# Low halves of the expert weights: summed by TensorE through identity matrices instead of subtracted by GpSimd, with eighteen places for raw slices

## The chip, the core and the metric

The kernel runs on one core of a Trainium2 chip. The metric is the device time of one execution in microseconds (us); smaller is better. Engines are named as in the profile: PE is TensorE (PEld its weight loads), DVE is VectorE, ACT is ScalarE, POOL is GpSimd, and SP is the engine whose queue issues most of the transfers.

## What is computed

There are two parts, one behind the other. The first is a linear recurrence with a complex decay for 4 batches, 8 heads, 768 steps and a head width of 48. The second is a two-layer network on the 3072 tokens that come out of it.

```python
mag = np.sqrt(a_re * a_re + a_im * a_im)
scale = np.minimum(mag, 0.999) / (mag + 1e-06)
...
for t in range(S):
    S_re, S_im = (ar * S_re - ai * S_im) + k_t v_t^T, ar * S_im + ai * S_re
    y[:, :, t] = q_t S_re
...
h = x @ w_in                      # 3072 x 384 by 384 x 2048
g = np.maximum(0.01 * h, h)
return g @ w_out                  # 3072 x 2048 by 2048 x 384
```

The two weight matrices come as 64-bit floats. The kernel converts them on the chip, and it wants about fp32 accuracy from matmuls in the `fp32r` type, which keeps fewer bits of a number. So every operand of the network is split in two, a high part `hi` in `fp32r` and a low part `lo` = value - `hi`, and each product is the sum of three: hi times hi, hi times lo, lo times hi.

## The kernel before

**The two stages.** Time is cut into 6 chunks of 128 steps, and each chunk into 2 pairs of batches: 12 sub-blocks `n`. For each one `prep(n)` builds the decayed queries and keys on DVE and ACT, from the raw tiles `a`, `qk` and `v`: normalising the decay (L468 to L484), products within groups of 8 steps (L489, L492, seven rounds), a scan over groups (L499 to L513), and the multiplication into `qkt` (L533 to L584). Transfers (L600 to L608) then turn `qkt` into the layout `t96` that TensorE needs (rows call it `t`). `attend` has four pieces for each sub-block, two for each batch: scores (`att<-t`, masked by DVE at L670 into `asb`) and the update of the running state, which ends in `xh` (ACT, L698) and `xl` (DVE, L701), the two halves of the network's input.

**The network.** `stream(g)` handles 256 tokens in 8 steps of 256 hidden columns. `first(g, s)` is 18 matmuls into `ph`; ACT (L752) and DVE (L753) make the leaky ReLU `tg`, ACT rounds it to `gh` (L754), DVE makes the remainder `gl` (L755). `second(g, s)` is 18 matmuls into `po`. The network of sub-block n-1 is laid out in one row of 16 or 18 steps, and the four attention pieces of sub-block n stand behind its steps 6, 8, 10 and 12. TensorE works through this row strictly in order, so a piece whose `t` is late stops the network matmuls behind it too.

**The weights.** There are 32 slices of 128 by 384, 16 of `w_in` and 16 of `w_out`, taken in turn. A slice is loaded raw (`stage_...<-in_w_dram`, 64 bits a number) into one of nine places, which are borrowed from tiles that are needed only later (`a`, `kn`, `xh`, `xl`, `stg`); from the ninth slice on the last three places rotate. Then `load_weights` does this with it:

- DVE L424 (`wcv<-stage`) shifts the upper word, DVE L428 puts the sign back: the number as an fp32 bit pattern, without its last 3 bits;
- ACT L431 takes these 3 bits from the lower word, and POOL L432 adds them;
- ACT L433 rounds the result to `fp32r` (`win_hi`, `wout_hi`), and POOL L434 subtracts that from it (`win_lo`, `wout_lo`).

`wcv` has two buffers. In the program's order the slices are spread over the preparation of sub-blocks 0, 1 and 2 on DVE. The order on each engine is set by a scheduler from priorities and a timeline of its own; TensorE's matmuls of the two stages keep the order in which they were written.

Of the kernel before, what the change touches and what calls it, by code (L numbers as in the profile page):

```python
# [9 lines left out]
I32 = mybir.dt.int32  # L10
U32 = mybir.dt.uint32
I64 = mybir.dt.int64
AF = mybir.ActivationFunctionType
# [7 lines left out]
P = 128  # L21
# [22 lines left out]

GAP = 2
TAIL = [1]
STAGES = [
    ("a", 3 * TI * 2 * C, 2), ("kn", H * 2 * D, 1), ("xh", TI * GT, 2), ("xl", TI * GT, 2), ("xh", TI * GT, 2),
    ("xl", TI * GT, 2), ("stg", 2 * DM, 1),
]  # L50
AHEAD = 4
EARLY = 8


def STAGE_OF(i):
    return i if i < 9 else 6 + i % 3

# [223 lines left out]
def body(ctx, tc, keep, a_in, qk_in, v_in, w_in, out):  # L281
# [23 lines left out]
    wacc = keep.tile([P, 2, WCP * -(-NWC // WCK)], F32, tag="wacc", name="wacc")  # L305

    def mm(out, **kw):
        tc.keep_in_program_order(nc.tensor.matmul(out, **kw))  # L308

    prio(PRIO_PREP)  # L310
    nc.scalar.preload_act_table_set("natural_log_exp_and_others")
    make_identity(nc, ident)


# [91 lines left out]
    def load_weights(lo, hi, base):  # L406
        prio(base)
        for f in range(lo, hi):
            for s in (f, NFC + f):
                i = s_next[0]  # L410
                st = weight_dma(i)
                cv = pp.tile([P, DM], I32, tag="cvt", name=f"wcv_{s}", bufs=2)
                s_next[0] += 1
                if s < NFC:
                    dh = win_hi[:, :, f * P : (f + 1) * P]
                    dl = win_lo[:, :, f * P : (f + 1) * P]
                else:
                    dh = wout_hi[:, f].rearrange("p (k x) -> p k x", k=TI)
                    dl = wout_lo[:, f].rearrange("p (k x) -> p k x", k=TI)
                words = st.rearrange("p (x two) -> p x two", two=2)  # L420
                uwords = st.bitcast(U32).rearrange("p (x two) -> p x two", two=2)
                hi_w, lo_w = words[:, :, 1], words[:, :, 0]
                wf = cv.bitcast(F32).rearrange("p (k x) -> p k x", k=TI)
                nc.vector.tensor_scalar(  # L424
                    out=cv.bitcast(U32), in0=uwords[:, :, 1], scalar1=5, scalar2=2,
                    op0=ALU.logical_shift_left, op1=ALU.logical_shift_right,
                )
                nc.vector.scalar_tensor_tensor(  # L428
                    out=hi_w, in0=hi_w, scalar=-(1 << 30), in1=cv, op0=ALU.bitwise_and, op1=ALU.bitwise_or
                )  # L430
                nc.scalar.activation(lo_w, uwords[:, :, 0], AF.Copy, scale=2.0**-29)  # L431
                nc.gpsimd.tensor_tensor(out=cv, in0=hi_w, in1=lo_w, op=ALU.add)  # L432
                nc.scalar.activation(dh, wf, AF.Copy)  # L433
                nc.gpsimd.tensor_tensor(out=dl, in0=wf, in1=dh.bitcast(F32), op=ALU.subtract)  # L434

# [196 lines left out]
    def attend(n, bi):  # L632
# [10 lines left out]
        def turn(hh):  # L643
            pt = att_bank()
            for h4 in range(4):
                tc.keep_in_program_order(
                    nc.tensor.transpose(
# [146 lines left out]
    for n in range(nsub + 1):  # L794
# [10 lines left out]
        if n > 0:  # L805
            order = stream(n - 1)
            for i, (what, g, s) in enumerate(order):
                what(g, s)
                left = len(order) - 1 - i
                while pieces and left <= GAP * len(pieces) + TAIL[min(n, len(TAIL) - 1)]:  # L810
                    pieces.pop(0)()
                    if left > 0:
                        break
                if n == nsub and left == 3:
                    prio(PRIO_FLAG)
                    bad = flag(nc, keep, pp, att_bank(), acc, zfl, wacc, xacc, low)
        for p in pieces:
            p()
    prio.save()
# [78 lines left out]
```

## Time and profile before

| what | value |
|---|---|
| time, median of 3 runs | 679.23 us (675.53 to 681.4) |
| the profiled execution's own time | 679.77 us, span 678.0 us |
| PE busy | 544.5 us, 80% of the span |
| DVE busy | 548.2 us, 81% |
| ACT busy | 368.6 us, 54% |
| POOL busy | 83.3 us, 12% |
| waits of PE for the transfer of `t`, whole span | 85.7 us, the first of them 73.0 us |

A share of the whole span is a mean over stages with different limits: PE has almost nothing to do in the first 79 us, and then works almost without a gap from 182 us on. So the page's row of forty slices, and the busy time by stage, say more than the totals. A duration in the timeline overlaps that of the next instruction on the same engine a little; the distance from start to start is what an instruction costs its engine.

### The profile page before, as it was taken

Reading aid. Unit: us, or ns where it says so; the run is one execution under the profiler, and the core shown is the slowest. Engines: PE = TensorE matmul, PEld = TensorE weight load, DVE = VectorE, ACT = ScalarE, POOL = GpSimd, SP = SyncE. Lnnn points to the kernel's source line nnn. Section 1 sums busy time; section 2 is a strip of 40 time slices with the busy share of each in tenths; the row PEclk is TensorE's granted clock in tenths of the full one; section 3 lists DMA queues with packets and bytes.
Section 4 is the critical chain, followed back from the end, with each engine's and each line's share of the span. In section 5 each row is a group of like instructions: output and inputs, shape, how many; then the busy total and the mean of one; then the engine's idle time right before and its main releaser. Section 6 shows DMA issues by size and latency. Waiting matters only on the chain.

```text
span 678.0 us, 17666 instructions
## 1 busy us (share of the span) xinstructions
PE 544.5 (80%) x7554; PEld 526.7 (78%) x7554; DVE 548.2 (81%) x917; ACT 368.6 (54%) x827; POOL 83.3 (12%) x75
## 2 busy tenths in 40 slices
PE   1000256668899999999999999999969998889996
PEld 0000245558899999999999999998969998889995
DVE  5989899979989999999998989979969876224231
ACT  6335166437557466574755747547446555657221
POOL 5665344541000000000000000000000000000000
PEclk9999977969999999999999999999989999999998
DMA  9223643370541603517045090370640763783000
GB/s 351 72 71 105 185 152 121 102 202 3 125 138 52 192 22 95 169 53 180 34 102 161 3 255 10 114 149 3 176 87 2 220 205 106 214 276 114 24 1 29
DMA packets 26246, 79.22 MB, mean 117 GB/s; under 512 B 3376, under 2 KB 9520, under 8 KB 26160
## 3 DMA queue, kind: packets, MB, share of 16 engines
q1 hardware_dynamic: 25552, 76.43, 38.3%
q10 hardware_dynamic: 608, 1.59, 1.1%
q8 instruction: 61, 1.00, 0.6%
q14 instruction: 25, 0.20, 0.1%
HBM read 54.26 MB, written 4.72 MB: 87 GB/s over the span
## 4 chain that ended last, share of the span: by engine, by line
DVE 38%; PE 26%; DMA 18%; issue 6%; ACT 6%; POOL 2%; SPq 1%; ACTq 0%; DVEq 0%; POOLq 0%
PE ph L308 11%; PE po L308 11%; DMA t<-qkt 10%; DMA wck<-in_w_dram 5%; PE att L308 4%; DVE tg L753 3%; DVE gl L755 3%; DVE tmp L489 3%; DVE asb L670 2%; DVE qkt L584 2%; DVE wcv L424 2%; DVE a L483 2%; DVE a L538 2%; DVE qkt L572 2%; DVE a L492 2%
## 5 line engine op out<-in xcount | busy, mean ns | idle before, releaser
L308 PE MATMUL ph<-xh,win_hi 128*128 128x256 f32 x576 | 165.2, 287 | 13.5 <-DVE tg L753 13.1
L308 PE MATMUL ph<-xl,win_hi 128*128 128x256 f32 x576 | 164.5, 286 | 3.5 <-DVE xl L701 3.5
L308 PE MATMUL ph<-xh,win_lo 128*128 128x256 f32 x576 | 164.0, 285 | 0.0
L308 PE MATMUL po<-gh,wout_hi 128*128 128x256 f32 x576 | 146.2, 290 | 3.4 <-ACT gh L754 3.4
L308 PE MATMUL po<-gh,wout_lo 128*128 128x256 f32 x576 | 141.4, 282 | 0.0
L308 PEld LDWEIGHTS ph<-xh,win_hi 128*128 128x128 f32 x576 | 110.7, 192 | 15.0 <-DVE tg L753 14.1
L308 PEld LDWEIGHTS po<-gh,wout_hi 128*128 128x128 f32 x576 | 109.8, 191 | 6.1 <-ACT gh L754 3.8
L753 DVE TENSOR_TENSOR tg<-ph,tg 128x512 f32<-128x512 f32 x96 | 65.6, 684 | 59.7 <-ACT tg L752 57.4
L308 PEld LDWEIGHTS ph<-xl,win_hi 128*128 128x128 f32 x576 | 110.8, 192 | 4.0 <-DVE xl L701 4.0
L308 PE MATMUL att<-t 96*32 96x64 f32 (+3 forms) x1536 | 41.4, 261 | 89.2 <-DMA t<-qkt 85.7
L308 PEld LDWEIGHTS ph<-xh,win_lo 128*128 128x128 f32 x576 | 110.8, 192 | 0.0
L308 PEld LDWEIGHTS po<-gh,wout_lo 128*128 128x128 f32 x576 | 109.9, 191 | 0.0
L308 PEld LDWEIGHTS att<-t 96*32 96x32 f32 x1536 | 35.5, 146 | 94.6 <-DVE a L492 73.4
L752 ACT ACTIVATE tg<-ph 128x512 f32<-128x512 f32 x96 | 56.8, 592 | 64.3 <-PE ph L308 63.9
L754 ACT CAST gh<-tg 128x512 fp32r<-128x512 f32 x96 | 59.3, 619 | 51.4 <-DVE tg L753 50.4
L308 PE MATMUL po<-gl,wout_hi 128*128 128x256 f32 x576 | 83.9, 281 | 1.3 <-DVE gl L755 1.3
L755 DVE TENSOR_TENSOR gl<-tg,gh 128x512 fp32r<-128x512 f32 x96 | 67.2, 700 | 12.1 <-ACT gh L754 11.9
L308 PEld LDWEIGHTS po<-gl,wout_hi 128*128 128x128 f32 x576 | 75.1, 190 | 1.7 <-DVE gl L755 1.7
L489 DVE TENSOR_TENSOR tmp<-a 128x384 f32<-128x384 f32 x84 | 51.4, 612 | 1.6
L308 PE MATMUL att<-asb,v 128*32 128x128 f32 x768 | 39.4, 287 | 5.7 <-DVE asb L670 5.7
L670 DVE TENSOR_TENSOR asb<-att,mask 128x512 f32<-128x512 f32 x48 | 32.1, 679 | 7.1 <-PE att L308 7.1
L729 ACT ACTIVATE rst<-rst,t 96x48 f32<-96x48 f32 x128 | 30.7, 323 | 13.1 <-DVE rst L722 13.0
(119 smaller groups left out, 884.0 us busy)
## 6 DMA issues: line engine op xcount, KB each, us to landing
t<-qkt SPq DMA_DIRECT2D x44, 290.2 KB, 6.3
wck<-in_w_dram SPq DMA_DIRECT2D x10, 1152.0 KB, 6.3
v<-in_v_dram SPq DMA_DIRECT2D x12, 832.0 KB, 5.3
a<-in_a_dram SPq DMA_DIRECT2D x12, 768.0 KB, 6.6
qk<-in_qk_dram SPq DMA_DIRECT2D x12, 768.0 KB, 4.6
out_dram<-ot SPq DMA_DIRECT2D x12, 384.0 KB, 4.3
stage_xh<-in_w_dram SPq DMA_DIRECT2D x10, 384.0 KB, 3.4
stage_xl<-in_w_dram SPq DMA_DIRECT2D x10, 384.0 KB, 3.1
```

What stands on the lines that cost most here:

```text
L308: tc.keep_in_program_order(nc.tensor.matmul(out, **kw))
L424: nc.vector.tensor_scalar(out=cv.bitcast(U32), in0=uwords[:, :, 1], scalar1=5, scalar2=2, op0=ALU.logical_shift_left, op1=ALU.logical_shif ...
L483: nc.vector.tensor_tensor(out=a[:, 1:3, sl], in0=a[:, 1:3, sl], in1=two(s0), op=ALU.mult)
L489: nc.vector.tensor_tensor(out=pr, in0=src.unsqueeze(2).to_broadcast([P, 2, 2, M]), in1=swap(ar, r), op=ALU.mult)
L492: nc.vector.tensor_tensor(out=zr[:, :, r], in0=pr[:, 0], in1=pr[:, 1], op=ALU.add)
L538: nc.vector.tensor_tensor(out=zk, in0=zk, in1=over_r(0), op=ALU.mult)
L670: nc.vector.tensor_tensor(out=asb, in0=ps, in1=mask, op=ALU.mult)
L729: nc.scalar.activation(r[:, h // 2, h % 2], src[:, h // 2, h % 2], AF.Copy, scale=t96[:, s0 + x, bi, C : C + 1])
L752: nc.scalar.activation(tg, ph, AF.Copy, scale=0.01)
L753: nc.vector.tensor_tensor(out=tg, in0=ph, in1=tg, op=ALU.max)
L754: nc.scalar.copy(gh, tg)
L755: nc.vector.tensor_tensor(out=gl, in0=tg, in1=gh.bitcast(F32), op=ALU.subtract)
```

## The change

All 32 slices are still split in two, but the sums are made elsewhere.

- POOL has no part in it: L432 and L434 are gone.
- DVE gets one instruction more for each slice (L447 in the changed file): it cuts the fp32 pattern down to its upper 20 bits and writes that over the raw upper word.
- ACT L448 writes the 3 bits of the lower word as one byte into the lowest byte of that same word; ACT L449 makes `hi` from it.
- PE makes the low part in PSUM with three matmuls of 384 columns: the identity (fp32) times the pattern, minus two times the identity (`nid`, fp32r) times `hi`, and the identity (fp32) times the cut pattern with its byte. The tile `pd` takes turns in the three banks that the network's `po` uses later.
- ACT copies `pd` to `win_lo` or `wout_lo` (L455).
- There are 18 places for raw slices, in place of 9: the tiles `qkt` and `t96` are borrowed as well, and the last five rotate. `wcv` has four buffers. `EARLY` goes from 8 to 14, which puts the first 14 slices ahead of the preparation in the order of the code.
- TensorE's matmuls of the two stages are kept in order by a chain of dependences; the new ones are not in that chain. The places of the attention pieces are now written as a table, and it names the steps 6, 8, 10, 12 again.

```diff
-GAP = 2
-TAIL = [1]
+PLACE = [(), (6, 8, 10, 12)]
 STAGES = [
-    ("a", 3 * TI * 2 * C, 2), ("kn", H * 2 * D, 1), ("xh", TI * GT, 2), ("xl", TI * GT, 2), ("xh", TI * GT, 2),
-    ("xl", TI * GT, 2), ("stg", 2 * DM, 1),
+    ("a", 3 * TI * 2 * C, 2), ("kn", H * 2 * D, 1), ("qkt", 4 * TI * 2 * (C + 1), 1), ("t96", 2 * H * 2 * (C + 1), 1),
+    ("xh", TI * GT, 2), ("xl", TI * GT, 2), ("xh", TI * GT, 2), ("xl", TI * GT, 2), ("stg", 2 * DM, 1),
 ]
+NST = 18
+NROT = 5
 AHEAD = 4
-EARLY = 8
+EARLY = 14
...
 def STAGE_OF(i):
-    return i if i < 9 else 6 + i % 3
+    return i if i < NST else NST - NROT + (i - NST) % NROT
...
     def mm(out, **kw):
-        tc.keep_in_program_order(nc.tensor.matmul(out, **kw))
+        chained(nc.tensor.matmul(out, **kw))
 
     prio(PRIO_PREP)
+    nid = cp.tile([P, P], F32R, tag="nid", name="nid")
...
+    nc.scalar.activation(nid, ident, AF.Copy, scale=-2.0)
...
-                cv = pp.tile([P, DM], I32, tag="cvt", name=f"wcv_{s}", bufs=2)
+                cv = pp.tile([P, DM], I32, tag="cvt", name=f"wcv_{s}", bufs=4)
...
-                hi_w, lo_w = words[:, :, 1], words[:, :, 0]
+                hi_w = words[:, :, 1]
+                r8 = st.bitcast(U8).rearrange("p (x b) -> p x b", b=8)[:, :, 4]
+                tf = st.bitcast(F32).rearrange("p (k x two) -> p k x two", k=TI, two=2)[:, :, :, 1]
...
                 nc.vector.scalar_tensor_tensor(
-                    out=hi_w, in0=hi_w, scalar=-(1 << 30), in1=cv, op0=ALU.bitwise_and, op1=ALU.bitwise_or
+                    out=cv, in0=hi_w, scalar=-(1 << 30), in1=cv, op0=ALU.bitwise_and, op1=ALU.bitwise_or
                 )
-                nc.scalar.activation(lo_w, uwords[:, :, 0], AF.Copy, scale=2.0**-29)
-                nc.gpsimd.tensor_tensor(out=cv, in0=hi_w, in1=lo_w, op=ALU.add)
-                nc.scalar.activation(dh, wf, AF.Copy)
-                nc.gpsimd.tensor_tensor(out=dl, in0=wf, in1=dh.bitcast(F32), op=ALU.subtract)
+
+                nc.vector.tensor_single_scalar(hi_w, cv, -(1 << 12), op=ALU.bitwise_and)
+                nc.scalar.activation(r8, uwords[:, :, 0], AF.Copy, scale=2.0**-29)
+                nc.scalar.activation(dh, tf, AF.Copy)
+                pd = pso.tile([P, 512], F32, tag=f"o{i % NOC}", name=f"pd_{s}")[:, 0:DM]
+                pd = pd.rearrange("p (k x) -> p k x", k=TI)
+                nc.tensor.matmul(pd, lhsT=ident, rhs=wf, start=True, stop=False)
+                nc.tensor.matmul(pd, lhsT=nid, rhs=dh, start=False, stop=False)
+                nc.tensor.matmul(pd, lhsT=ident, rhs=tf, start=False, stop=True)
+                nc.scalar.copy(dl, pd)
```

Two places show what this does to the order on the engines. The first is DVE around the last two instructions of `prep(0)`, those that finish `qkt` and let the transfers of `t` go (L584, in the changed file L605). Before:

```order
L483 TENSOR_TENSOR a_282<-a_282,tmp_676 128x1536
L579 TENSOR_TENSOR qk_133<-qk_133,a_132 128x768
L424 TENSOR_SCALAR wcv_345<-stage_xh_129 128x384
L424 TENSOR_SCALAR wcv_353<-stage_xl_130 128x384
L584 TENSOR_TENSOR qkt_244<-qk_133,a_132 128x6x128 x2
L489 TENSOR_TENSOR tmp_676<-a_282 128x384
L428 SCALAR_TENSOR_TENSOR stage_xh_129<-stage_xh_129,wcv_345 128x384
```

Now:

```order
L504 TENSOR_TENSOR a_390<-a_390,tmp_808 128x1536
L443 SCALAR_TENSOR_TENSOR wcv_565<-stage_xh_131,wcv_565 128x384
L600 TENSOR_TENSOR qk_137<-qk_137,a_136 128x768
L443 SCALAR_TENSOR_TENSOR wcv_577<-stage_xl_132,wcv_577 128x384
L439 TENSOR_SCALAR wcv_589<-stage_xh_133 128x384
L439 TENSOR_SCALAR wcv_601<-stage_xl_134 128x384
L447 TENSOR_SCALAR stage_xh_131<-wcv_565 128x384
L510 TENSOR_TENSOR tmp_808<-a_390 128x384
L605 TENSOR_TENSOR qkt_352<-qk_137,a_136 128x6x128 x2
L447 TENSOR_SCALAR stage_xl_132<-wcv_577 128x384
L443 SCALAR_TENSOR_TENSOR wcv_589<-stage_xh_133,wcv_589 128x384
```

In the first order 17 of the 32 first steps (L424) and 15 second steps (L428) stand ahead of the end of `qkt`, and the other slices behind it, as far as the middle of `prep(2)`. In the second all 32 first steps (L439), 30 second steps (L443) and 29 of the new third steps (L447) stand ahead of it, and the last five instructions on weights right behind.

The second place is PE between the transposes of the first attention block (`att<-ident,t`) and the products with the masked scores (`att<-asb,v`). Before:

```order
L647 MATMUL att_99<-ident,t_0_271 128x96 x4
L647 MATMUL att_100<-ident,t_0_271 128x96 x4
L308 MATMUL att_101<-asb_0_0_498,v_134 32x128 x6
```

Now:

```order
L668 MATMUL att_101<-ident,t_0_379 128x96 x4
L668 MATMUL att_102<-ident,t_0_379 128x96 x4
L453 MATMUL pd_595<-win_hi,nid 128x384
L454 MATMUL pd_595<-stage_xh_133,ident 128x384
L453 MATMUL pd_607<-wout_hi,nid 128x384
L454 MATMUL pd_607<-stage_xl_134,ident 128x384
L319 MATMUL att_103<-asb_0_0_630,v_138 32x128 x6
```

`pd_607` is the last slice: 29 of the 32 low parts are summed on PE ahead of the first attention matmul, three end among those of the first batch, and none stands in the network's part of the row, whose order is as before.

## Rows read from the trace of the kernel before

**Rows 1.** The page, busy time of each engine, and DVE in 40 slices of the span (tenths busy).

```profile
PE 544.5 (80%) x7554; PEld 526.7 (78%) x7554; DVE 548.2 (81%) x917; ACT 368.6 (54%) x827; POOL 83.3 (12%) x75
...
DVE  5989899979989999999998989979969876224231
```

**Rows 2.** Busy time by stage: the stretch (us from the span's start), its length, busy us of PE, PEld, DVE, ACT and POOL with numbers of instructions, then PE's granted clock (1.00 is 2.4 GHz, 0.50 is 1.2 GHz), the share of the DMA engines and GB/s.

```profile
6.15:73.00 66.85, 0.04 (x4) 0.00 (x0) 60.45 (x84) 30.99 (x62) 40.27 (x30) 1.00 0.37 131
73.00:106.80 33.80, 15.00 (x306) 12.29 (x306) 30.19 (x53) 17.29 (x48) 13.85 (x14) 0.81 0.61 184
106.80:140.80 34.00, 19.53 (x133) 18.49 (x133) 33.23 (x45) 16.34 (x33) 18.70 (x13) 0.80 0.46 122
140.80:182.00 41.20, 35.44 (x494) 33.37 (x494) 38.09 (x61) 23.49 (x61) 6.93 (x7) 0.91 0.29 94
182.00:560.00 378.00, 368.30 (x5400) 360.48 (x5401) 344.46 (x601) 223.21 (x520) 0.00 (x0) 0.99 0.40 111
```

**Rows 3.** What PE waited for from 100 to 200 us: us in total, times, the longest.

```profile
PE att L308 <- DMA t<-qkt: 10.6, 1, 10.6
PE ph L308 <- DVE tg L753: 3.3, 2, 3.2
PE ph L308 <- DVE xl L701: 3.2, 1, 3.2
```

**Rows 4.** The timeline: start, us, engine, line, what was done, and in brackets the idle time before it and what ended it. The last writes to `qkt` of sub-block 0, the first scores, the first full run of network matmuls, the first scores of sub-block 1.

```profile
71.22 1.81 DVE L584 TENSOR_TENSOR qkt<-qk,a 128x768 f32<-128x768 f32 x2
...
79.16 0.61 PE L308 MATMUL att<-t 96*32 96x128 f32 x8 [72.97 <-DMA t<-qkt]
...
106.79 0.58 PE L308 MATMUL ph<-xl,win_hi 128*128 128x256 f32 x1 [3.15 <-DVE xl L701]
...
140.09 0.64 PE L308 MATMUL att<-t 96*32 96x128 f32 x8 [10.55 <-DMA t<-qkt]
```

**Rows 5.** Groups of DVE instructions, busy us in total and mean ns of one. The first two rows are from 6 to 73 us, the others from 182 to 560 us.

```profile
L489 DVE TENSOR_TENSOR tmp<-a 128x384 f32<-128x384 f32 x8 | 7.4, 930 | 0.1
...
L428 DVE SCALAR_TENSOR_TENSOR stage_xl<-stage_xl,wcv 128x384 int32<-128x384 int32 x4 | 2.2, 547 | 0.0
...
L489 DVE TENSOR_TENSOR tmp<-a 128x384 f32<-128x384 f32 x61 | 33.7, 553 | 1.2
...
L506 DVE TENSOR_TENSOR tmp<-xs 128x360 f32<-128x360 f32 (+3 forms) x36 | 16.6, 462 | 2.7 <-ACT xs L498 1.5
...
L538 DVE TENSOR_TENSOR a<-a 128x1536 f32<-128x1536 f32 x9 | 15.8, 1752 | 0.0
...
L512 DVE TENSOR_TENSOR xs<-tmp 128x90 f32<-128x90 f32 (+3 forms) x36 | 8.4, 232 | 0.9
```

**Rows 6.** The timeline of DVE, two neighbours each, at moments when POOL does nothing.

```profile
70.68 0.35 DVE L424 TENSOR_SCALAR wcv<-stage_xh 128x384 uint32<-128x384 uint32 x1
70.95 0.35 DVE L424 TENSOR_SCALAR wcv<-stage_xl 128x384 uint32<-128x384 uint32 x1
...
204.28 0.95 DVE L539 TENSOR_TENSOR a<-a,qkt 128x768 f32<-128x768 f32 x1
205.15 0.95 DVE L540 TENSOR_TENSOR a<-a,qkt 128x768 f32<-128x768 f32 x1
```

**Rows 7.** What DVE waited for up to 110 us (the longest entry), and one POOL instruction of the timeline.

```profile
DVE wcv L424 <- POOL win_lo L434: 5.5, 3, 2.3
...
44.21 5.49 POOL L432 TENSOR_TENSOR wcv<-stage_xl 128x384 int32<-128x384 int32 x1 [2.23 <-issue]
```

**Rows 8.** Records of PE. The first three are fp32 matmuls of 128 columns (ns shortest/median/longest, first and last start in us; each instruction of the program leaves two records). The others are from the timeline (start, us): the network's fp32r matmuls of 256 columns, one record each, and one of their weight loads.

```profile
L341 PE MATMUL att<-perm x32: 420/421/421, 4.3 to 5.8; 128*32 128x128 f32 x32
...
L308 PE MATMUL att<-asb,v x32: 419/421/421, 99.4 to 100.9; 128*32 128x128 f32 x32
...
L308 PE MATMUL att<-asb,v x28: 270/272/297, 299.8 to 329.9; 128*32 128x128 f32 x28
...
107.39 0.41 PE L308 MATMUL ph<-xh,win_hi 128*128 128x256 f32 x1
107.60 0.41 PE L308 MATMUL ph<-xl,win_hi 128*128 128x256 f32 x1
...
107.39 0.33 PEld L308 LDWEIGHTS ph<-xl,win_hi 128*128 128x128 f32 x1
...
111.05 0.28 PE L308 MATMUL ph<-xh,win_hi 128*128 128x256 f32 x1
111.17 0.29 PE L308 MATMUL ph<-xl,win_hi 128*128 128x256 f32 x1
```

**Rows 9.** Short stretches with PE's granted clock (columns as in rows 2).

```profile
5.00:6.00 1.00, 1.00 (x24) 0.69 (x16) 0.00 (x0) 0.78 (x1) 0.00 (x0) 1.00 1.00 381
...
99.00:101.00 2.00, 1.59 (x32) 1.48 (x35) 2.00 (x4) 1.20 (x3) 0.61 (x1) 0.50 0.03 12
...
106.80:110.80 4.00, 4.00 (x18) 4.00 (x19) 4.00 (x5) 1.97 (x3) 2.51 (x2) 0.50 0.62 234
...
152.00:154.00 2.00, 0.93 (x48) 0.79 (x36) 1.93 (x4) 1.28 (x4) 2.00 (x3) 1.00 0.03 8
```

**Rows 10.** Groups of ACT instructions, whole span: the work on a lower word from SBUF, and a copy of 384 columns out of PSUM.

```profile
L431 ACT ACTIVATE stage_xh<-stage_xh 128x384 int32<-128x384 uint32 x10 | 5.6, 556 | 7.5 <-DMA stage_xh<-in_w_dram 7.5
...
L653 ACT COPY kn<-att 128x384 f32<-128x384 f32 x40 | 18.8, 472 | 3.9 <-PE att L647 3.9
```

More of the change, by code (lines that the diff above doesn't have):

```diff
@@ L11 @@
 U32 = mybir.dt.uint32
+U8 = mybir.dt.uint8
 I64 = mybir.dt.int64
@@ L305, in body, with chained @@
     wacc = keep.tile([P, 2, WCP * -(-NWC // WCK)], F32, tag="wacc", name="wacc")
+    chain = []
+    after = mybir.DependencyInfo(mybir.DependencyClass.NoSync, mybir.DependencyReason.DATA)
+    def chained(x):
+        if chain:
+            tc.add_manual_dep(x.ins, chain[-1].name, after, reason="chained")
+        chain.append(x.ins)
     def mm(out, **kw):
-        tc.keep_in_program_order(nc.tensor.matmul(out, **kw))
+        chained(nc.tensor.matmul(out, **kw))
     prio(PRIO_PREP)
+    nid = cp.tile([P, P], F32R, tag="nid", name="nid")
     nc.scalar.preload_act_table_set("natural_log_exp_and_others")
     make_identity(nc, ident)
+    nc.scalar.activation(nid, ident, AF.Copy, scale=-2.0)
     perm = pp.tile([P, 2, C], F32, tag="asb", name="perm", bufs=2)
@@ L645, in turn @@
             for h4 in range(4):
-                tc.keep_in_program_order(
+                chained(
                     nc.tensor.transpose(
@@ L808, in body @@
                 what(g, s)
-                left = len(order) - 1 - i
-                while pieces and left <= GAP * len(pieces) + TAIL[min(n, len(TAIL) - 1)]:
+                for _ in range(PLACE[min(n, len(PLACE) - 1)].count(i) if pieces else 0):
                     pieces.pop(0)()
-                    if left > 0:
-                        break
-                if n == nsub and left == 3:
+                if n == nsub and i == len(order) - 4:
                     prio(PRIO_FLAG)
                     bad = flag(nc, keep, pp, att_bank(), acc, zfl, wacc, xacc, low)
-        for p in pieces:
-            p()
+        if n == 0:
+            for p in pieces:
+                p()
     prio.save()
```

## Prediction

> **What bounds the kernel now.** I read the busy totals first, then the stages, then what ends PE's waits, and only then single instructions. The totals put PE and DVE side by side [rows 1], but they bind in different places. From 182 to 560 us PE is busy 368.3 of 378 us [rows 2]: there the network's matmuls set the pace, and a microsecond won earlier reaches the end. Before that it is DVE. From 6.15 to 73 us DVE is busy 60.45 of 66.85 us and PE does nothing [rows 2]; at 73.0 us (71.22 + 1.81) `qkt` of the first sub-block is done, the first scores start at 79.16 and the network runs from 106.79 [rows 4]. From there to 182 us PE is idle 14.5 + 5.8 us (34.00 - 19.53 and 41.20 - 35.44), and it runs at a mean clock of 0.80 and 0.91 [rows 2]. Its longest wait is 10.6 us for the `t` of sub-block 1, with 3.3 us for `tg` and 3.2 for `xl` behind [rows 3], and `t`, `tg` and `xl` all come from DVE, which is busy 33.23 of the 34.00 us in which most of this lies [rows 2].
>
> Why is DVE so full? While POOL works, a step of 384 columns (L489) takes 930 ns; without POOL it takes 553 [rows 5]. POOL is busy 40.27 of the 66.85 us [rows 2], and DVE also stands still 5.5 us in three waits for it [rows 7].
>
> **What DVE costs up to the end of `qkt`.** A DVE instruction's successor starts about 0.08 us ahead of its recorded end (0.95 long, 0.87 from start to start) [rows 6], so I take durations from stretches without POOL, less 0.08. The preparation that stands ahead of this point is: 18 instructions of 768 columns at 0.87, 15.7 us; 4 of 1536 at 1.67, 6.7; 8 of L489 at 0.47, 3.8 [rows 5, 6]; 7 of 192 columns at 0.27 (I take them like L424), 1.9; the scan, 4 at 0.38 and 8 at 0.15, 2.7 [rows 5], with tiny ones 3.1. That is 31.2 us. Before, 17 L424 at 0.27 [rows 6] and 15 L428 at 0.47 [rows 5] add 11.6: 42.8 us of work in a stretch of 66.85, so some 24 us are stretched instructions and waits.
>
> Now 32 first steps (8.6 us) and 30 second steps (14.1) stand there, and 29 of the new third step. No row shows that form with a spaced output: it lies between the shift (0.27) and the two-input step (0.47), 7.8 to 13.6 us; I take the middle, 10.7. Sum 31.2 + 33.4 = 64.6 us, and from 6.15 us that ends at 70.8. For waits I take 6 us, as many as DVE's idle time before (66.85 - 60.45): POOL's go, but DVE now follows PE and ACT through four `wcv` buffers and the slots. So `qkt` is done at **77 us**, 4 later than before; with neither waits nor the dearer form it is 68.
>
> **ACT and the transfers.** ACT's third instruction on each slice, a copy out of PSUM, costs about 0.43 us [rows 10]; with a byte output, which no row shows, I take the same for L448 as for L431. Before it was busy 30.99 of 66.85 us [rows 2] with about 30 weight instructions in it; 85 at some 0.45 us put 25 us more on it, 56 of 71 us. It hides behind DVE as long as PE answers in time; without that cover each late `pd` holds the `prep` steps queued behind its copy, which is what my 6 us pay for. The raw slices load earlier, into 18 places, and all weight transfers are issued ahead of those of `t`, so SP's queue is no longer than before.
>
> **PE's new work.** An fp32 record of 128 columns lasts 421 ns where an fp32r record of 256 columns lasts 410, and 272 where that lasts 280 [rows 8]. So I count an fp32 record as two passes and the instruction, with its two records, as four. The network's spacing is 0.21 us per 256 columns at the lower level and 0.12 at the upper [rows 8]. 384 columns then cost 1.28 or 0.71 us in fp32, 0.32 or 0.18 in fp32r, and a slice 2.9 or **1.6 us**. The nearest row bounds this from both sides: 16 fp32 instructions of 128 columns, each 32 rows of output wide, take 1.93 us (their records start over 1.5 us and last 0.42) [rows 8], 0.36 us per 384 columns if they run one behind another and 1.45 if four run at a time.
>
> Which level? The trace shows 1.00 at 5 us [rows 9], but the records there are 421 ns long, as at 99.4 us [rows 8], where it shows 0.50 [rows 9]; so the engine starts at the lower level, 1.2 GHz. Four microseconds of unbroken matmuls ended that at 110.8 us, and a stretch with PE busy 0.93 of 2 us stayed at 1.00 [rows 9]. DVE delivers a slice every 2.2 us (71 us / 32). At 2.9 us PE falls behind and is never idle, which raises its clock; at 1.6 it is busy 70%, more than in that stretch. So I take the upper level for most slices, and PE hides behind DVE. The Trainium skill ("TensorE: Matmul & The Clock Gate", Part 1) names 1.2 GHz as the state of an idle engine, and warns that the clock events of a trace can be unreliable. By that rule the 421 ns decide, as above; by the 1.00 as printed every slice would cost 1.6 us from the start, and the second rival below would not exist.
>
> **From `qkt` to the network.** Before this took 33.8 us (106.79 - 73.0), DVE busy 30.19 of them [rows 2]. Now the DVE work up to the second `xl` is five leftover weight steps (2.1), 6 L489 and 7 L492 (4.7), the scan (3.1), two of 1536 (3.3), nine of 768 (7.8), four masks of 512 columns at 0.6 and two `xl` at 0.47 (3.3): 24.3 us. The transfer of `t` comes first as before (6 us, 73.0 to 79.16) [rows 4], and three late slices stand among the first scores on PE; I take **31 us**, between 27 and 34. The network starts at 77 + 31 = 108, one later than before.
>
> **In the network's first 75 us.** No weight work is left for DVE. After the second `xl` it needs about 7.6 us to the end of `qkt` of sub-block 1, and the transfer 7: `t` arrives at 77 + 46. PE gets to it after five `first` and two `second`, 126 matmuls: 36 at mostly the lower level, about 6 us, a wait for `tg` of about 3 that stays, and 90 at 0.12, 10.8, in all 31 + 20 = 77 + 51. So the 10.6 us wait goes, and nothing takes its place at that point. Before, idle time was 20.3 us, and the lower level cost about 6.6 more (some 13 us of matmuls at half pace, from the mean clocks [rows 2]): 27 us. I keep 11: the `tg` wait 3, a slow start 2, smaller waits for `kn`, `gh` and `gl` 4, the clock 2. Gain 16.
>
> **Sum.** 679.8 + 4 (`qkt`) - 3 (to the network) - 16 (its first 75 us) = 664.8 us for the profiled execution, which lies 0.5 above the median of the runs: **664 us**. The order of the network's row and its attention steps are unchanged, so the placement table costs and gains nothing, and PE is full from 182 us on to carry the gain to the end.
>
> **The rivals.**
>
> 1. *Nothing waits.* The third step costs 0.27 and PE and ACT always answer in time: `qkt` at 68, and the later stage keeps only 8 us. 679.8 - 5 - 3 - 19 = 653, near 652 by the median. For it: DVE's other idle time before is small [rows 7]. Against it: three engines in order, each more than half full.
> 2. *PE stays at 1.2 GHz.* Then PE sets the pace: 28 slices at 2.9 us from 8 us on, `qkt` at 89, 12 later than forecast: 676. For it: it starts at that level. Against it: the 0.93 of 2 us at full clock [rows 9].
> 3. *The long DVE steps are not POOL's doing*, but for instance that of the transfers; then the 18 us of stretching stay: about 682. Against it: the transfers' share is the same 0.37 and 0.40 in both stretches [rows 2] and L489 is 553 in one of them [rows 5]. The Trainium skill ("GPSIMD Engine Reference", Key points) says that POOL shares its SBUF interfaces with DVE; by that this rival falls, and the rows agree (930 and 553 ns).
> 4. *Slower: PE's weight loads show.* A slice has five loads of 128 by 128, 0.33 us each at the lower level [rows 8]. If half of them are not hidden, a slice costs 3.7 us, DVE waits for a free `wcv`, `qkt` ends at 112, and the time is 679.8 + 39 - 3 - 16 = 700. The sign turns at `qkt` 92, that is 3.0 us a slice; 1% slower is 3.25. Against it: in the network the loads lie wholly beside the matmuls (0.21 from start to start with a load of 0.33 in each) [rows 8].
>
> **How the numbers follow.** Chances: forecast 0.66 (656 to 672), rival 1 0.11, rival 2 0.12, rival 3 0.04, rival 4 0.07. The likeliest time is 664. The range goes from 653, which takes in most of rival 1, to 679, which takes in rival 2; rival 4 and half of rival 3 are left out. One percent, about what a measurement of this kernel tells from no change, is 6.8 us. Faster by more: forecast, rival 1 and a little of rival 2, 0.79. Within 1%: most of rival 2 and rival 3, 0.14. Slower: rival 4, 0.07.
>
> **What would show it.** Right: POOL idle after 5 us; L510 near 0.55 us throughout; `qkt` finished at 73 to 82; first scores of sub-block 1 near 128 with no wait of several microseconds before them; PE busy above 85% from 108 to 182. Rival 2 shows as fp32 records of about 1.1 us for 384 columns up to the first scores, rival 4 as PE idle between `pd` matmuls with a load ahead of each. The forecast is wrong if DVE waits often for PE or ACT before `qkt`, or if a wait for `t` of sub-block 1 or 2 comes back.

## The result, and the profile after

The changed kernel takes **654.41 us** (median of 4 runs, 652.7 to 655.94); the kernel before took 679.75 us beside it. The ratio is 0.9636, with a 95% interval from 0.9585 to 0.9686: 25 us, or 3.6%, faster. The forecast was 664, its range 653 to 679. The profile is of the run of 655.94 us, its span 653.9.

The page of the changed kernel: busy time of each engine, then DVE and ACT in 40 slices of the span (answers to [rows 1]).

```profile
PE 597.7 (91%) x7714; PEld 551.4 (84%) x7714; DVE 523.0 (80%) x949; ACT 394.2 (60%) x860; POOL 3.6 (1%) x11
...
DVE  4989869899899998998999989979979776324231
ACT  7899748376384674855746647456465546747321
```

POOL is done after its start-up. PE has 53 us more to do, DVE 25 us less. The share of PE rises mainly because the first 80 us, in which it stood, now hold the sums.

Busy time by stage, columns as in [rows 2]. The cuts are the end of `qkt` of sub-block 0, the start of the network, and 182 us as before.

```profile
6.15:80.00 73.85, 53.23 (x150) 25.34 (x147) 62.71 (x144) 67.09 (x115) 0.00 (x0) 1.00 0.54 194
80.00:110.65 30.65, 19.56 (x319) 13.41 (x318) 24.89 (x47) 18.20 (x42) 0.00 (x0) 0.62 0.38 105
110.65:182.00 71.35, 69.03 (x914) 67.23 (x917) 65.59 (x119) 38.53 (x96) 0.00 (x0) 0.97 0.43 120
182.00:560.00 378.00, 370.72 (x5445) 362.63 (x5435) 340.79 (x587) 228.20 (x529) 0.00 (x0) 0.99 0.40 109
```

The timeline at the four moments of [rows 4]: last write to `qkt`, first scores, first network matmul, first scores of sub-block 1.

```profile
78.14 1.82 DVE L605 TENSOR_TENSOR qkt<-qk,a 128x768 f32<-128x768 f32 x2
...
86.19 0.61 PE L319 MATMUL att<-t 96*32 96x128 f32 x8 [3.79 <-DMA t<-qkt]
...
110.65 0.58 PE L319 MATMUL ph<-xh,win_hi 128*128 128x256 f32 x1
...
130.34 0.88 PE L319 MATMUL att<-t 96*32 96x128 f32 x32
```

`qkt` is ready at 79.96 us (78.14 + 1.82), 6.9 later than before. The network starts 30.7 us behind it, 3.9 later than before (110.65 against 106.79). And then the gain comes all at once: the scores of sub-block 1 start at 130.34 in place of 140.09, without a wait, and those of sub-block 2 at 173.30 in place of 192.88. Of PE's 71.35 us from 110.65 to 182 only 2.3 are idle, at a mean clock of 0.97. Of PE's waits from 100 to 200 us, these are the three longest (answers to [rows 3], where 10.6 us for `t` led):

```profile
PE att L319 <- DVE xl L722: 3.5, 1, 3.5
PE ph L319 <- DVE tg L774: 2.1, 1, 2.1
PE att L319 <- DVE asb L691: 1.9, 1, 1.9
```

The spans differ by 24.1 us, and this is where it lies: `qkt` +6.9, from there to the network -3.1 (30.7 against 33.8), from the network's start to sub-block 2 -23.4 (62.7 against 86.1 us), and behind that -4.5.

The instructions of the first stage, from 6 to 80 us (busy us and mean ns): the step that POOL used to stretch [rows 5], a step four times as long, the new third step of DVE, and the byte step of ACT, which answers to L431 in [rows 10].

```profile
L510 DVE TENSOR_TENSOR tmp<-a 128x384 f32<-128x384 f32 x8 | 4.4, 556 | 0.0
L504 DVE TENSOR_TENSOR a<-a,tmp 128x1536 f32<-128x1536 f32 x2 | 3.5, 1757 | 0.0
...
L447 DVE TENSOR_SCALAR stage_xh<-wcv 128x384 int32<-128x384 int32 x7 | 2.5, 358 | 0.0
...
L448 ACT ACTIVATE stage_xh<-stage_xh 128x384 uint8<-128x384 uint32 x7 | 7.5, 1065 | 1.2 <-DVE stage_xh L447 1.2
```

L510 has the 0.55 us of a stretch without POOL; the third step costs as little as the shift. The byte step takes **1065 ns where the word took 556**. ACT's timeline shows one slice from byte step to byte step, and then a byte step that the copy follows at once:

```profile
37.31 1.08 ACT L448 ACTIVATE stage_xh<-stage_xh 128x384 uint8<-128x384 uint32 x1
38.42 0.56 ACT L449 ACTIVATE wout_hi<-stage_xh 128x384 fp32r<-128x384 f32 x1
38.88 0.46 ACT L455 CAST wout_lo<-pd 128x384 fp32r<-128x384 f32 x1
39.24 1.07 ACT L448 ACTIVATE stage_xl<-stage_xl 128x384 uint8<-128x384 uint32 x1
...
41.17 1.07 ACT L448 ACTIVATE stage_xh<-stage_xh 128x384 uint8<-128x384 uint32 x1
41.98 0.58 ACT L455 CAST wout_lo<-pd 128x384 fp32r<-128x384 f32 x1
```

The byte step costs ACT 0.81 us (41.98 - 41.17), and 1.11 where `hi`, which reads its result, comes next (38.42 - 37.31). A whole slice costs 1.93 (39.24 - 37.31), and ACT is busy 67.09 of 73.85 us. What DVE waited for from 6 to 80 us:

```profile
DVE wcv L439 <- DMA stage_a<-in_w_dram: 4.2, 1, 4.2
DVE wcv L439 <- PE pd L452: 2.9, 4, 1.5
DVE tmp L503 <- ACT tmp L500: 2.8, 1, 2.8
DVE tmp L527 <- ACT xs L519: 2.6, 1, 2.6
```

The first of these waits began at 2.1 us and ended at 6.3, so it lies almost wholly ahead of the stretch (the kernel before has it too, 4.0 us). Of the 11.1 us that DVE is idle from 6.15 to 80 us, six waits for ACT make 7.5 and four for PE 2.9; the rest is loads.

### The profile page after: what moved, and what is told of

Its sections match the earlier page's. It is cut to its first block, busy times and chain, and to the rows that moved or that the text cites. A ratio compares the mean times of both kernels' runs of the same rounds, so it can differ in the third digit from the quotient of the medians.

```text
span 653.9 us, 18010 instructions
## 1 busy us (share of the span) xinstructions
PE 597.7 (91%) x7714; PEld 551.4 (84%) x7714; DVE 523.0 (80%) x949; ACT 394.2 (60%) x860; POOL 3.6 (1%) x11
## 4 chain that ended last, share of the span: by engine, by line
PE 34%; DVE 28%; DMA 21%; ACT 10%; issue 4%; SPq 1%; ACTq 0%; DVEq 0%
PE po L319 14%; PE ph L319 14%; DMA t<-qkt 10%; DMA wck<-in_w_dram 6%; PE att L319 4%; DVE asb L691 2%; DVE tg L774 2%; DVE a L504 2%; DVE gl L776 2%; DVE a L559 2%; ACT wck L416 2%; ACT wck L417 2%; DVE qkt L593 2%; DMA a<-in_a_dram 2%; DMA stage_qkt<-in_w_dram 1%
## 5 line engine op out<-in xcount | busy, mean ns | idle before, releaser
L319 PE MATMUL po<-gh,wout_hi 128*128 128x256 f32 x576 | 144.1, 287 | 3.8 <-ACT gh L775 3.8
L319 PE MATMUL po<-gh,wout_lo 128*128 128x256 f32 x576 | 139.5, 279 | 0.0
L319 PEld LDWEIGHTS po<-gh,wout_hi 128*128 128x128 f32 x576 | 108.1, 188 | 6.4 <-ACT gh L775 4.2
L319 PEld LDWEIGHTS po<-gh,wout_lo 128*128 128x128 f32 x576 | 108.2, 188 | 0.0
L319 PE MATMUL att<-t 96*32 96x128 f32 (+3 forms) x1536 | 39.7, 259 | 9.0 <-DMA t<-qkt 5.5
L510 DVE TENSOR_TENSOR tmp<-a 128x384 f32<-128x384 f32 x84 | 46.6, 555 | 1.3
L452 PE MATMUL pd<-wcv,ident 128*128 128x384 f32 x64 | 30.0, 567 | 12.3 <-DVE wcv L443 6.1
L750 ACT ACTIVATE rst<-rst,t 96x48 f32<-96x48 f32 x128 | 30.7, 322 | 13.7 <-DVE rst L743 13.7
```

The costliest lines, as they stand in the source:

```text
L319: chained(nc.tensor.matmul(out, **kw))
L452: nc.tensor.matmul(pd, lhsT=ident, rhs=wf, start=True, stop=False)
L510: nc.vector.tensor_tensor(out=pr, in0=src.unsqueeze(2).to_broadcast([P, 2, 2, M]), in1=swap(ar, r), op=ALU.mult)
L750: nc.scalar.activation(r[:, h // 2, h % 2], src[:, h // 2, h % 2], AF.Copy, scale=t96[:, s0 + x, bi, C : C + 1])
```

## Experiments

Three questions stood. Is it POOL's absence that makes DVE faster, or the places? How much does PE's part give, and is it free? And why did the late part of the program gain 4.5 us that nobody foretold? All kernels differ from the changed kernel, if not said otherwise; each was compared with runs of the kernel before on its chip (677.6 to 679.7 us).

### The eighteen places alone

The kernel before, POOL still summing, with the new places, `EARLY` and four `wcv`:

```diff
-EARLY = 8
+NST, NROT, EARLY = 18, 5, 14
...
-    return i if i < 9 else 6 + i % 3
+    return i if i < NST else NST - NROT + (i - NST) % NROT
```

> The kernel before, POOL still summing, with only the 18 places, EARLY 14 and four wcv buffers of the change. 25 of 32 slices stand ahead of the first qkt. Theory 'POOL stretches DVE': the more slices run beside prep(0), the more it is stretched; qkt at 83 to 93 us in place of 73, L489 still near 0.9 us in that stretch, and what is won later is lost here: 670 to 684 us. Rival 'the places are the gain': 654 to 662 us.

Measured: 684.39 us, ratio 1.0077 (1.0052 to 1.0102). That is just beyond the far end of what the POOL theory allowed, and 22 us from its rival. More slices run early, and their POOL work with them; DVE's 384-column step from 6 to 75 us (stretched, but less than the 0.9 us expected) and the end of `qkt`:

```profile
L491 DVE TENSOR_TENSOR tmp<-a 128x384 f32<-128x384 f32 x7 | 5.0, 721 | 0.1
...
87.48 3.24 DVE L586 TENSOR_TENSOR qkt<-qk,a 128x768 f32<-128x768 f32 x2
```

`qkt` ends at 90.7, 17.7 us later than before. By sub-block 2 all but 3.2 of that is won back (its first products with masked scores start at 202.66 us, before at 199.43), since fewer slices are left for the later stages. With POOL still summing the places are worth nothing.

### POOL's work put back, unread

```diff
+    dmy = cp.tile([P, 2, P], F32, tag="dmy", name="dmy")
+    two_id = ident.unsqueeze(1).to_broadcast([P, 2, P])
+    for _ in range(60):
+        nc.gpsimd.tensor_tensor(out=dmy, in0=two_id, in1=two_id, op=ALU.subtract)
```

> The changed kernel with 60 extra POOL subtractions of 256 columns from the start, whose result nobody reads and which wait for nothing but the identity. Theory 'POOL's work stretches DVE': before, 40 us of POOL work cost DVE some 18 us, 0.45 us each; here 45 to 60 us of POOL work bring L510 from 0.55 to about 0.9 us, qkt from 80 to about 92 to 100 us, and the time to 664 to 678 us. Rival 'the long DVE steps were the transfers' doing': L510 stays at 0.55 and the time at 653 to 656 us.

Measured: 671.63 us (ratio 0.9891, 0.9833 to 0.9948), inside the expectation. DVE's work up to `qkt` is that of the changed kernel (144 instructions), and its steps are longer again, beside subtractions that nobody reads. Three groups from 6 to 75 us (the two-input step of 384 columns, the shift, the step of 1536 columns), and the stretch up to the end of `qkt`:

```profile
L514 DVE TENSOR_TENSOR tmp<-a 128x384 f32<-128x384 f32 x7 | 5.9, 848 | 0.0
...
L443 DVE TENSOR_SCALAR wcv<-stage_qkt 128x384 uint32<-128x384 uint32 x4 | 3.0, 766 | 0.0
...
L508 DVE TENSOR_TENSOR a<-a,tmp 128x1536 f32<-128x1536 f32 x1 | 2.2, 2168 | 0.0
...
6.15:96.60 90.45, 58.78 (x150) 27.83 (x147) 85.33 (x144) 68.44 (x115) 42.25 (x58) 0.92 0.46 159
```

`qkt` ends at 96.61, 16.7 us later. Ahead of it POOL was busy 42.25 us, and DVE 22.6 us longer than in the changed kernel (85.33 against 62.71); 6 us of that it took from its own idle time. So **one microsecond of POOL delayed `qkt` by 0.39 us**. The price is one per instruction of DVE, not per column: the shift takes 0.77 us in place of 0.36, the two-input step 0.97 in place of 0.56 while POOL works (848 ns is a mean that takes in steps after POOL's end), the step of 1536 columns 2.17 in place of 1.76, each time 0.41 us more. The whole time is 17.2 us longer, so all of the delay reaches the end, and the stretching is POOL's doing; the forecast's third rival (transfers) falls. The Trainium skill ("Trainium Architecture — The Big Picture", What this means for kernel authors) says that DVE and GpSimd contend for a shared pair of ports, by an exclusive lock and not by a split of bandwidth. The runs agree that they contend, and the same 0.41 us on a short and on a long step fits turns at a lock better than a split, by which the long step would lose more; how long either engine holds it no run shows.

### The low part made by DVE, not by PE

```diff
-                nc.vector.tensor_single_scalar(hi_w, cv, -(1 << 12), op=ALU.bitwise_and)
-                nc.scalar.activation(r8, uwords[:, :, 0], AF.Copy, scale=2.0**-29)
-                nc.scalar.activation(dh, tf, AF.Copy)
...
-                nc.scalar.copy(dl, pd)
+                nc.scalar.activation(lo_w, uwords[:, :, 0], AF.Copy, scale=2.0**-29)
+                nc.vector.tensor_tensor(out=cv, in0=cv, in1=lo_w, op=ALU.bitwise_or)
+                nc.scalar.activation(dh, wf, AF.Copy)
+                nc.vector.tensor_tensor(out=dl, in0=wf, in1=dh.bitcast(F32), op=ALU.subtract)
```

> The changed kernel without PE in the weights: DVE puts the 3 bits in (a two-input step of 0.47 us in place of the cut of 0.27) and subtracts hi itself (0.47 more), ACT writes a word in place of a byte and copies nothing out of PSUM (0.8 us less a slice). Theory, DVE sets the pace up to qkt: 0.67 us by 29 slices is 19 us more of DVE, of which its waits of 11 us take some back; qkt ends at 88 to 97, 664 to 673 us. Rival, ACT set the pace: its relief pays for DVE's work and qkt ends by 83, 650 to 658 us.

Measured: 666.59 us (ratio 0.9861, 0.9823 to 0.9899), as the first theory had it. `qkt` ends at 91.91, and up to there DVE is hardly ever idle:

```profile
6.15:91.90 85.75, 0.04 (x4) 0.00 (x0) 84.95 (x181) 46.67 (x93) 0.00 (x0) 1.00 0.48 167
```

It is 9 to 12 us faster than the kernel before (by the ratio and by the medians) and 12 to 15 slower than the changed kernel. So of the 25 us somewhat under half come from taking the sums off POOL with eighteen places, even if DVE makes them, and the rest from giving them to PE (with the byte step on ACT that this needs).

### PE's work made longer

```diff
+                nc.tensor.matmul(pd, lhsT=ident, rhs=wf, start=True, stop=True)
                 nc.tensor.matmul(pd, lhsT=ident, rhs=wf, start=True, stop=False)
```

> The changed kernel with the first identity matmul of each slice done twice (the first result is overwritten): 0.67 to 0.7 us more on PE for each slice, some 20 us in all up to the end of qkt, where PE was idle 20.6 of 73.85 us. Theory, PE lies beside DVE and ACT, and its cover is some 20 us thick in sum but thin slice by slice: qkt ends 2 to 8 us later, 656 to 664 us. Rival, PE was part of the pace already (ACT's copy waits for it): qkt 15 us or more later, 668 us or more.

Measured: 656.25 us (ratio 0.9697, 0.9659 to 0.9735), at the near end of the theory: some 20 us more on PE cost the whole little or nothing (1.8 us by the medians, within the intervals). But the way there was not the expected one. The scheduler found another order, with the preparation ahead of more slices:

```profile
67.13 1.82 DVE L606 TENSOR_TENSOR qkt<-qk,a 128x768 f32<-128x768 f32 x2
...
75.77 0.61 PE L319 MATMUL att<-t 96*32 96x128 f32 x8 [3.45 <-DMA t<-qkt]
```

`qkt` was ready 11 us *earlier* than in the changed kernel, and the full run of network matmuls started only 2 us earlier (108.52 us), since the rest of the slices then stood among the first attention. The end of `qkt` is a marker of one order, not by itself a measure of the gain.

### A word in place of the byte

```diff
-                nc.vector.tensor_single_scalar(hi_w, cv, -(1 << 12), op=ALU.bitwise_and)
-                nc.scalar.activation(r8, uwords[:, :, 0], AF.Copy, scale=2.0**-29)
+                nc.scalar.activation(lo_w, uwords[:, :, 0], AF.Copy, scale=2.0**-29)
+                nc.vector.scalar_tensor_tensor(
+                    out=hi_w, in0=cv, scalar=-(1 << 12), in1=lo_w, op0=ALU.bitwise_and, op1=ALU.bitwise_or
+                )
```

> The changed kernel, but ACT writes the 3 bits as a 32-bit word into the lower word (as L431 did), and DVE joins them with a two-input step in place of the cut (L447). Theory 'ACT sets the pace of the first 80 us, through its byte output of 0.80 us from start to start': ACT is relieved by about 0.35 us a slice, 11 us, DVE gets 0.2 more, 6 us; qkt ends at 74 to 78 us and the time is 648 to 653 us. Rival, the prediction's reading that DVE sets it: qkt at 84 to 87 us, 657 to 662 us.

Measured: 660.72 us (ratio 0.9733, 0.9678 to 0.9788). The stretch up to the end of `qkt`, and the first scores of sub-block 1:

```profile
6.15:82.00 75.85, 56.44 (x164) 29.05 (x160) 70.22 (x148) 58.44 (x125) 0.00 (x0) 0.94 0.54 189
...
130.05 1.52 PE L319 MATMUL att<-t 96*32 96x128 f32 x64
```

`qkt` ended at 82.0, only 2 us later and between the two expectations. DVE's busy time rose by 7.5 us, to 70.22 (its new step is dearer, and all 32 slices stand ahead of `qkt`), but its idle time fell from 11.1 to 5.6, and its waits for ACT and PE from 10.5 to 2.0. (Its waits for raw slices rose from 0.6 to 3.6.) So ACT's dear byte costs DVE some 5.5 us of waiting on balance, and DVE and ACT set the pace together. The time is that of the DVE theory, but by another way: the scores of sub-block 1 start no later than in the changed kernel (130.34), so what the time is longer by arises behind them, and these rows do not show why.

### Nine places with PE summing, and a chase after its slow middle

```diff
-NST, NROT, EARLY = 18, 5, 14
+EARLY = 8
...
-    return i if i < NST else NST - NROT + (i - NST) % NROT
+    return i if i < 9 else 6 + i % 3
```

> The changed kernel with the nine places of before and EARLY 8 again; sums on PE, none on POOL, wcv with four buffers. In its order 19 of 32 slices stand ahead of the end of the first qkt on DVE, 13 behind. Theory 'all conversions ahead of the network are part of the gain': qkt of sub-block 0 ends at 60 to 68 us in place of 80, but 13 slices go beside prep(1) and the network, the waits for tg and for t of sub-block 1 partly come back: 658 to 665 us. Rival 'POOL's absence is the whole gain, the places add nothing': 653 to 656 us.

Measured: 709.07 us (ratio 1.0408, 1.0327 to 1.0489), 44 us beyond the far end of the expectation and slower than the kernel before. The start is about as expected (`qkt` at 69.1, the first network matmul at 100.3). But slices are converted until some 144 us, in the network's stretch, and their sums stand there in PE's row. Of PE's waits from 100 to 200 us, 13.2 us are at the sums themselves. The longest entry:

```profile
PE pd L450 <- DVE wcv L441: 5.9, 4, 2.0
```

By sub-block 2 the kernel is 28 us behind the changed one (its first products with masked scores start at 207.91 us, in the changed kernel at 179.88). The other half of the loss comes later: from sub-block 2 to 9 the sub-blocks are 47.9 us apart, where the changed kernel needs 44.2. One sub-block, in order of time: DVE's last write to `qkt`, the last matmuls and the last ACT copies that read the `t` of the sub-block ahead, the first transfer of the new `t`, DVE's first write to the next `qkt`, and PE.

```profile
214.18 1.81 DVE L603 TENSOR_TENSOR qkt<-qk,a 128x768 f32<-128x768 f32 x2
...
223.30 0.86 PE L317 MATMUL att<-v,kn 128*32 128x48 f32 x48
...
225.94 1.92 ACT L748 ACTIVATE rst<-rst,t 96x48 f32<-96x48 f32 x8 [1.53 <-DVE rst L741]
...
227.88 2.21 SPq L619 DMA_DIRECT2D t<-qkt  x2
...
239.48 1.76 DVE L552 TENSOR_TENSOR qkt<-a 128x1536 f32<-128x1536 f32 x1 [2.98 <-DMA t<-qkt]
...
242.76 0.97 PE L317 MATMUL po<-gl,wout_hi 128*128 128x256 f32 x6 [4.09 <-DVE gl L774]
```

`qkt` is ready at 216, but `t` has one buffer, and its readers are not done until 227.9. The transfers then hold `qkt` until 239.5, DVE waits in front of its next write to it, and `gl`, queued behind, comes late for PE. From 182 to 560 us DVE stood 36.8 us there, in the changed kernel 10.9.

Two edits moved that first write. One kept the products `tb` in `tmp`:

```diff
-        tb = qkt[:, :, 1].rearrange("p l i b t -> p l (i b t)")[:, :, :N]
+        tb = tmp[:, 0:2]
```

> Nine places as in nine_places, and one edit in prep: the products tb are kept in tmp and no longer in half of qkt, so that the next preparation first writes to qkt some 10 us later. Theory: nine_places took 709 us because in its order DVE reaches that first write of qkt (L552) before the transfers out of qkt are done; it waited 36.8 us there between 182 and 560 us, the tg and gl behind it were late, PE stood some 28 us after 182 us and ran at half clock after each wait. Without it: 662 to 678 us, DVE waits for t<-qkt and out_dram<-ot under 8 us from 182 to 560. Rival, the few places or the early network make the steady part slow by other means (the clock, other transfers): 695 us or more, sub-blocks still some 49 us apart.

> The changed kernel with the same one edit (tb in tmp). The changed kernel's PE waits after 200 us sum to 10.8 us (4.1 of them at 529 us), DVE waits 10.9 us for the transfers at L554 from 182 to 560. Theory, those late waits come from the first write of qkt: they go, with the lower clock behind them, 640 to 648 us. Rival, they come from elsewhere, or the scan then waits for tmp: 651 us or more.

Measured: 735.05 us with nine places (ratio 1.0836, 1.0781 to 1.0891) and 733.50 with eighteen (1.0821, 1.0791 to 1.0851). The wait at `qkt` is gone, and a dearer one took its place, in the eighteen-place kernel from 182 us on:

```profile
PE att L319 <- DMA t<-qkt: 52.4, 19, 15.7
```

`tmp` is now held to the end of a preparation, so the next normalisation cannot run ahead, which is the likely reason why `t` is late 19 times. The other edit put `tb` of sub-blocks 1 to 11 into the place of `wcv`, which is free by then:

```diff
+    wcv = pp.tile([P, 4, DM], I32, tag="cvt", name="wcv")
...
+        if n > 0:
+            tb = pp.tile([P, 2, N], F32, tag="cvt", name=f"tb_{n}")
```

> nine_places again, with tb of sub-blocks 1 to 11 in the place of wcv (free by then, 4 by 384 words), so that neither qkt nor tmp is held: DVE's first write to qkt comes some 10 us later and the next normalisation may still run ahead. Theory as before: the 49 us sub-blocks of nine_places come from DVE waiting at its first write to qkt for the transfers out of it (36.8 us from 182 to 560). Then 660 to 680 us, sub-blocks 44 to 46 us apart, DVE waits for t<-qkt and out_dram<-ot under 8 us. Rival, with nine places the steady part is slow by other means: 695 us or more.

> The changed kernel with tb of sub-blocks 1 to 11 in the place of wcv, nothing else. Theory, the late PE waits of the changed kernel (10.8 us after 200 us, and some 4 us of half clock behind them) come from the first write to qkt: 640 to 649 us, PE waits after 200 us under 5 us. Rival, the order that the scheduler finds is worse, as with tb in tmp, where PE waited 52 us for t: 660 us or more. Third, the late waits have other causes: 651 to 657 us.

> The kernel before with the same edit (wcv keeps its two places, tb of sub-blocks 1 to 11 beside it). Its late PE waits are 15.7 us after 200 us, its DVE waits for the transfers at L533 14.7. Theory, the part of the gain that nobody foretold (25.3 measured, 20 at sub-block 2) is these waits and not the weights: with them gone in both kernels 662 to 670 us here, and 18 to 22 us between the two. Rival, the 5 us belong to the weights: 674 us or more here, or over 24 us between the two.

Measured: nine places 715.27 us (1.0545), the changed kernel 653.80 (0.9624, 0.9580 to 0.9667, so no change), the kernel before 709.31 (1.0449). The first theory falls. With nine places DVE still waited 20.1 us for the transfers from 182 to 560 us, now at its later first write, and the sub-blocks stayed 47.7 us apart. In the changed kernel the late waits stayed about as long. The third is no fair test: there the slices are spread as far as `prep(2)`, `tb` of sub-block 1 gets its place only behind the last of them, and PE stood 40 us at the place where it stood 10.6 before:

```profile
162.78 0.61 PE L308 MATMUL att<-t 96*32 96x128 f32 x8 [40.18 <-DMA t<-qkt]
```

So what the nine-place kernel suffers from is not that one tile. DVE's fixed order runs there a phase ahead of PE's row, and whatever it meets first (`qkt`, or behind it `t`) stops it with `tg` and `gl` queued behind. That is a reading of the rows; no run moved the phase alone. Why the scheduler finds that order with nine places, and not with eighteen, stays open.

### The late waits

PE's waits of the changed kernel after 200 us, the two largest:

```profile
PE ph L319 <- DVE tg L774: 4.1, 1, 4.1
PE po L319 <- ACT gh L775: 3.8, 2, 2.8
```

All its late waits sum to 11.3 us, those of the kernel before to 16.9 (of which 9.7 for `tg`): a difference of 5.6 us, about the 4.5 us of gain behind sub-block 2. One of them was tried by itself. At 506.31 us a load of the last weight check stands ahead of the transfers of `t` on SP's queue (with a load of `v` at 506.79 between them; the first transfer of `t` starts at 510.37):

```diff
-            nc.sync.dma_start(out=st[:, :ns], in_=w_in[s0 : s0 + ns].rearrange("s p x -> p s x"))
+            nc.gpsimd.dma_start(out=st[:, :ns], in_=w_in[s0 : s0 + ns].rearrange("s p x -> p s x"))
```

> The changed kernel with the 11 loads of the last weight check (wck, L410) issued by POOL's queue in place of SP's, nothing else. In the changed kernel one of them stands right ahead of the transfers of t at 506.31 us, DVE then waits 5.32 us for those at L554 and PE 4.10 at 529.07. Theory A, the queue: wck loads hold SP's queue and t behind them; that DVE wait falls below 3 us, PE's below 2.5, 648 to 652 us. Theory B, the DMA engines (they are busy the whole of 510 to 525 us): the wait stays at 5 us or so, 653 to 656 us. Theory C, POOL's issuing disturbs DVE: 658 us or more.

Measured: 657.85 us (ratio 0.9709, 0.9681 to 0.9737). The waits of 5.32 us (DVE) and 4.10 us (PE) are gone from the list, but not as theory A has it. The first write of DVE to `qkt` behind these transfers, in the changed kernel and in this one:

```profile
526.56 1.76 DVE L554 TENSOR_TENSOR qkt<-a 128x1536 f32<-128x1536 f32 x1 [5.32 <-DMA t<-qkt]
...
527.39 1.76 DVE L554 TENSOR_TENSOR qkt<-a 128x1536 f32<-128x1536 f32 x1
```

It comes 0.8 us later, not earlier. DVE no longer waits there, because it arrives late itself. The transfers of `t` started 0.7 us earlier (509.65 us), and the DMA engines' share is 1.00 or more from 510 to 525 us in both kernels, as theory B has it for the transfers. PE now waits elsewhere, and ACT for the loads:

```profile
518.69 0.58 PE L319 MATMUL po<-gh,wout_hi 128*128 128x256 f32 x1 [3.00 <-ACT gh L775]
...
575.76 0.49 PE L319 MATMUL po<-gh,wout_hi 128*128 128x256 f32 x1 [4.65 <-ACT ot L799]
...
516.82 1.21 ACT L416 ACTIVATE wck<-wck 128x1152 f32<-128x1152 f32 x1 [6.72 <-DMA wck<-in_w_dram]
```

The first is plain: ACT's next instruction but one is that `gh` (518.03 us), and it stood behind a step that waited 6.72 us for such a load; DVE's `gl` behind it waited 5.12 us. The time is near that of theory C, but these waits, and not DVE's speed, are what the rows show. The waits moved rather than went. None of the kernels tried is measurably faster than the changed one.

## Why the prediction held, and where it did not

- **What bounds the start.** That POOL stretches DVE is shown (0.97 us beside POOL's work, 0.56 without). That DVE alone sets the pace held only where it makes the sums itself (`low_by_dve`, busy 84.95 of 85.75 us). In the changed kernel DVE is busy 62.71 of 73.85 us and ACT 67.09, and they set it together. "It hides behind DVE as long as PE answers in time" did not hold for ACT, and the forecast's own sign of being wrong, that DVE waits often for PE or ACT before `qkt`, came: ten waits, 10.5 us.
- **`qkt` at 77.** It was 79.96, with two terms off in opposite directions, so that it came so near is in part luck. The work of DVE was put at 64.6 us and came to 62.7, mainly since the third step costs 0.27 us, the lower bound, and not 0.37. The waits were put at 6 and came to 11. The failing step is "I take the same for L448 as for L431": the byte step costs ACT 0.81 us or more, not 0.45, and 29 of them fill ACT to 67.09 of 73.85 us, where 56 of 71 had been counted. With the word in its place (`word_for_byte`) the waits are 5.6 us, which is the forecast's 6.
- **PE at 1.6 us a slice, at the upper level, beside DVE.** Right, rivals 2 and 4 did not come. Six records of the first slices took 4.15 us, some 0.67 apart, as at 1.2 GHz; behind that run two took 0.81 to 0.84:

```profile
8.47 4.15 PE L452 MATMUL pd<-wcv,ident 128*128 128x384 f32 x6 [2.28 <-DVE wcv L443]
...
16.66 0.81 PE L452 MATMUL pd<-wcv,ident 128*128 128x384 f32 x2
17.26 0.44 PE L453 MATMUL pd<-wout_hi,nid 128*128 128x384 f32 x1
17.54 0.83 PE L454 MATMUL pd<-stage_kn,ident 128*128 128x384 f32 x2
```

  From 16.66 to 17.26 two records and the step to the next instruction take 0.60. That PE is mostly hidden, `pe_twice` supports, in another order; slice by slice it is not wholly so, for 2.9 us of DVE's waits end with PE.
- **31 us from `qkt` to the network.** Measured 30.7.
- **"I keep 11" of idle time and slow clock in the network's first 75 us.** This is the term that was most off. Idle 2.3 us and about 2 us of clock (0.97 of 71.35 us) are left, 4.5 in place of 11. The wait for `tg` came (2.1 for 3); the smaller ones for `kn`, `gh` and `gl`, taken over from before at 4 us, and the slow start at 2 nearly all went. The likely reason is that no weight step stands in DVE's queue any more. `nine_places`, which has them in this stretch again, fits that, but there the sums stand in PE's row too, so the reason is not shown by itself.
- **"PE is full from 182 us on to carry the gain to the end."** It carried it, and 4.5 us more came, out of late waits that the forecast took as equal on both sides. Which late waits a version gets hangs on the order that the scheduler finds; the runs above moved them and brought no gain.
- **Sum.** +3 for `qkt`, -6.5 for the network's first stretch, -4.5 for what lies behind it: the forecast's 664.8 for the profiled execution becomes 656.8; it took 655.94. The errors of the later stages, 11 us together, all fell on the side of the gain. The time lies near that of the first rival (653), but not by its way: its `qkt` at 68 did not come.
- That the table of places and the chain cost nothing was read from the unchanged order, and not run by itself.

## What to carry to other kernels

Work taken off POOL pays where DVE is the bound: beside POOL's stream every DVE instruction, short or long, was 0.41 us longer, so count the instructions. DVE's waits for POOL go as well, but others can take their place, here those for ACT. An idle TensorE can take sums and differences at little cost while it has nothing else to do; the steps around it (here ACT's) want pricing in their real output type first. And a freed engine pays where its queue was the cause of several waits, so count the small waits behind the large one as well; but with in-order queues and one buffer a change elsewhere can shift the phase between two engines, and cost more than it saved.

## What was not expected of the hardware

- An ACTIVATE of 384 columns that writes bytes, 8 bytes apart, takes 1065 ns, and one that writes words at the same distance 556. Whether it is the type or the place of the byte, no run separates.
- POOL's two-input subtractions of 256 columns, although nobody reads them, make each DVE instruction beside them 0.41 us longer, at 384 columns as at 1536.
- PE's records kept the spacing of the upper level across a gap of 1.93 us ahead of 20.30 us (two records in 0.88 behind it). The profile's clock reads 1.00 also for the first six records, which by their distance ran at 1.2 GHz.
